# Two of eight batches get their transposed x from VectorE block turns of a second copy, and the whole order is searched anew

## The chip, the cores and the metric

One NeuronCore of one Trainium2 chip runs the kernel as one launch. The metric is the device time of one execution in microseconds (us). Engines are named as the profile names them: PE (TensorE matmul), PEld (its weight load), DVE (VectorE), ACT (ScalarE), POOL (GpSimd), SP (SyncE, which here only issues DMAs).

## What is computed

```python
# x: (8, 8, 512, 64) f32   state: (8, 8, 32, 64) f32
scores = x @ state^T / 8;   a  = softmax(scores);   xread = a @ state
scores2 = state @ x^T / 8;  a2 = softmax(scores2);  sread = a2 @ x
rows = concat([xread, sread], axis=2)          # per batch 544 rows of 8 * 64 = 512
# mixture of depths, per batch:
s = rows @ w_gate                              # 544 scores
top = the 128 rows with the largest s
out[top] = rows[top] + sigmoid(s[top]) * (relu(rows[top] @ w1) @ w2)   # w1: 512x1024, w2: 1024x512
out[others] = rows[others]
```

Both scores of a batch come from one product, x times state transposed; its two softmaxes run along its two axes.

## The kernel before

All work is recorded as 769 pieces by `add(engine, length, fn, after=..., takes=..., uses=...)`. A piece is a few instructions on one engine, with the pieces it needs and the buffers it takes or uses. `carry_out()` then issues the pieces in the order of the table `PLAN`: an entry `122:0:2` is piece 122, its first choice of engine, and buffer number 2 for what it takes. An entry `w:9:7` issues nine "identity turns": transposes of the identity matrix into PSUM bank 7 whose result nobody reads. Each engine runs its own instructions strictly in that order, and waits where an input is not ready. The lengths given to `add` are not used at run time.

Per batch, `attention(b)` does this:

- `load_x` brings x of the batch into one of the `xf` buffers (two DMAs of 512 KB on SP). x is needed in two forms: as it lies (in `state_read`, line 681), and turned, so that the head dimension lies on the partitions (in `scores`, line 516).
- `turn` (line 492) turns x on PE, four 128x128 transposes for each of the four pairs of heads, into a PSUM bank, and `keep` copies the bank into an `xT` buffer, on ACT (line 499) or DVE (line 497).
- `scores` (line 516) makes the scores in two PSUM banks. DVE takes the maximum along one axis (`s_max`, line 546), turns the scores in blocks of 32x32 into `e` (`turn_in`, line 531), takes the other maximum (`x_max`, 534), subtracts (`x_sub`, 537), and after ACT's exponential turns back into `eT` (`turn_out`, 543).
- `read` (line 620, twice per batch) makes xread; `keep` scales it into `xs`, per half a DVE piece of one instruction (line 631) or an ACT piece of eight (line 636); SP stores it (line 645). `turn_a`, `keep_a` and `state_read` (lines 662, 668, 681) make sread; SP stores it (line 691).

`choice(b)` then ranks the 544 scores (`row_x` 738, `win` 754, `wins_over` 779, `one_hot` 788, `pick` 806), fetches the 128 chosen rows by an indirect DMA on POOL (`fetch`, 816) and makes the sigmoid. `layers` runs the two layers for batches 0 and 7 alone (lines 905, 925), and `layers_of_two` for the pairs (1,2), (3,4), (5,6) with seven products of half matrices in place of eight (lines 992, 1099), for which POOL forms sums of the weights (line 415). `put` adds the results to the rows in `out` by an indirect DMA on POOL (line 868).

`ON_DVE` names batches whose x is to be turned by DVE, and is empty before. For such a batch `load_x2` brings a second copy of x by four SP DMAs, each into 32 partitions, in runs of 32 elements (128 bytes) so that 32x32 block turns (`turn_blocks`, four per batch, 512 columns each) give `xT` directly; `turn` and its `keep` fall away.

The state of all batches lies in one buffer, `stb`. Before, it holds one of the five `xf` buffers until the last reader of it is done.

Of the kernel before, what the change touches and what calls it, by code (L numbers as in the profile page):

```python
# [8 lines left out]
F32 = mybir.dt.float32  # L9
# [10 lines left out]
0:0:0 16:0:0 1:0:1 4:0: 3:0: 5:0: 2:0: 11:0: 7:0:2 6:0: 8:0: 20:0: 9:0:3 w:10:7 42:0:0 44:0:1 10:0: 43:0: 17:0: 14:0:  # L20
45:1:0 50:0:2 12:0:4 51:0:1 48:0:0 13:0: 49:1:2 46:0:1 18:0: 47:0:3 w:4:7 52:0:0 21:0: 57:0: 19:0: w:6:7 122:0:2 22:0:
53:0:0 182:0:3 24:0: 123:0:0 25:0: 124:0:4 54:0: 58:0:0 w:2:7 126:0:2 59:0: 55:0: 125:0:1 w:5:7 76:0:0 74:0:1 30:0:
56:0: 26:0: 128:0:4 61:0: 183:0: 60:0:0 129:0:2 77:0:0 27:0: w:9:7 68:0:4 31:0: 127:0:3 28:0: 75:0:1 184:0:0 69:0:
130:0:2 70:0: 185:0:4 71:1:0 78:0:0 135:0: 72:0: 190:0:1 372:0:1 131:0:0 35:0: 191:0:0 w:2:7 62:0:4 73:0: 79:0: 132:0:
136:0:0 188:0:1 80:0: 186:0:0 81:0: 189:0:1 63:0: 36:0: 64:0: 187:0:2 65:1:1 137:0: w:7:3 192:0:0 133:0: 66:0: 370:0:2
34:0: 82:0:3 139:0: 83:0: 193:0:1 152:0:3 134:0: 310:0:4 67:0: 373:0: 84:0:6 197:0: 85:0: 153:0:0 23:0: 154:0:5 91:0:
374:0:3 86:0:0 155:0:1 371:0: 314:0:5 87:0: 156:0:2 315:0:0 88:0: 198:0:0 89:0: 556:0:2 90:0: 138:0:0 199:0: w:2:7
92:0:5 15:0: 312:0:6 375:0:1 214:0:7 93:0: 94:0:0 215:0:0 194:0: w:3:7 95:0:5 157:0: 308:0:7 313:0:2 158:0: 146:0:0
97:0: 309:0:3 195:0: 98:0:0 96:0: 378:0:6 311:0:4 216:0:7 147:0: 99:0: 316:0:4 217:0:1 149:1:0 196:0: 148:0: 376:0:7
150:1: 379:0:0 321:0: w:2:6 140:0:0 377:0:2 558:0:6 141:0: 322:0:0 218:0:7 143:1:1 559:0:3 40:0: 142:0: 679:0:3 323:0:  # L30
# [13 lines left out]
401:1:0 570:0: w:4:3 326:0:0 402:1: 403:0: 283:0:4 327:0: 328:0: 284:0: 574:0:0 412:0:5 348:0:6 289:0:0 413:0: 278:0:2  # L44
# [28 lines left out]
def kernel(  # L73
# [37 lines left out]
    ON_DVE = ()  # L111
# [51 lines left out]
    def add(engine, length, fn, after=(), takes=(), uses=(), key=(), lands=0.0, moves=0.0):  # L163
        options = [(engine, length)] if isinstance(engine, str) else list(zip(engine, length))
        go = (lambda e: fn()) if isinstance(engine, str) else fn
        pieces.append(Piece(options, go, after, takes, uses, key, lands, moves))
        return pieces[-1]
# [38 lines left out]
    R_X = Ring("xf", [128, H, NC, D], F32, 5)  # L206
# [108 lines left out]
    def load_x(b, pieces=2):  # L315
        buf = xf[b] = Buf(R_X)
        n = H // pieces
        p_x[b] = []
        for h in range(0, H, n):

            on = "ACT" if b == 0 and h + n == H else "SP"

            def go(h=h, on=on):
                queue = nc.scalar if on == "ACT" else nc.sync
                queue.dma_start(out=buf.ap[:, h:h + n], in_=x[b, h:h + n].rearrange("h (p c) d -> p h c d", c=NC))

            p_x[b].append(add(on, 0.6, go, takes=[] if h else [buf], uses=[buf] if h else [], key=(b, "load_x"),
                              lands=2.0, moves=3.3 / pieces))
# [138 lines left out]
    def attention(b):  # L467

        def key(n):
            return (b, n)  # L470
# [121 lines left out]
        else:  # L592
            p = add("DVE", 1.25, turn_in, after=[p_s], takes=[e], uses=[s], key=key("in"))
            p = add("DVE", 1.2, x_max, after=[p] + four_ago, uses=[e], key=key("max"))
            p = add("DVE", 1.22, x_sub, after=[p], uses=[e], key=key("sub"))
# [114 lines left out]
    def choice(b, p_sc, p_xt, p_st):  # L710

        def key(n):
            return (b, n)
# [83 lines left out]
        for k, (lo, hi) in enumerate(slot_tiles):  # L797
# [55 lines left out]
            u["got"] = add("POOL", 1.25, fetch, after=[p] + all_stores, takes=[u["xr"]], key=key("fetch"), lands=3.0, moves=0.9)  # L853
# [351 lines left out]
```

## Time and profile before

| | |
|---|---|
| runs shown | 212.14, 215.03, 216.16 us; median 215.03 |
| profiled execution | 213.38 us, of which the span from the first to the last instruction is 211.6 us |
| mean granted PE clock | 0.990 |
| busy in the span | PE 196.9, PEld 169.4, DVE 143.3, ACT 95.4, POOL 81.6 us |

Busy time of PE is modelled from the starts of pipelined matmuls, so stretches are compared by when PE moves on, and by what its idle time waited for.

### The profile page before, as it was taken

The page shows a single profiled execution, that of the slowest core. Times are in us where ns is not written, and L with a number is a line of the kernel's source. Part 1 is how long each engine was busy: PE and PEld are TensorE (multiplying, and loading weights), DVE is VectorE, ACT ScalarE, POOL GpSimd, SP SyncE. Part 2 cuts the span into 40 slices and gives each one's busy share as a digit, 9 for nine tenths or more (in the row PEclk, how much of TensorE's full clock was granted, in tenths as well). Part 3 has the DMA queues.
Part 4 walks back from the last instruction along what each step waited for, and adds up shares of the span by engine and source line. Part 5 has one row for each costly group of instructions (what it writes and reads, how often), then busy time and mean ns, then how long its engine had stood idle before and what let it go on. Part 6 is the DMA issues. An engine that isn't in the chain of part 4 may idle for free.

```text
span 211.6 us, 6083 instructions
## 1 busy us (share of the span) xinstructions
PE 196.9 (93%) x2472; PEld 169.4 (80%) x2472; DVE 143.3 (68%) x378; ACT 95.4 (45%) x266; POOL 81.6 (39%) x174
## 2 busy tenths in 40 slices
PE   5988889887999999999999999999999999999990
PEld 4976657776987587998887889998888898989980
DVE  0389999879979978778977896798778342621000
ACT  2347876776276656213626776474133222130200
POOL 8220970507704839910521530500325327015404
PEclk9999999999699999999999999999999999999999
DMA  6999745969843301322231440431334303494501
GB/s 192 297 370 383 262 126 166 288 213 292 290 133 113 135 12 41 50 103 102 104 112 53 149 65 15 112 84 61 136 127 149 50 5 58 62 304 100 74 0 50
DMA packets 20324, 28.77 MB, mean 136 GB/s; under 512 B 5384, under 2 KB 14856, under 8 KB 20296
## 3 DMA queue, kind: packets, MB, share of 16 engines
q1 hardware_dynamic: 17344, 23.73, 33.5%
q0 software_dynamic: 1888, 4.20, 10.7%
q10 hardware_dynamic: 1064, 0.46, 0.8%
q8 instruction: 19, 0.31, 0.6%
q14 instruction: 9, 0.07, 0.1%
HBM read 17.37 MB, written 11.01 MB: 134 GB/s over the span
## 4 chain that ended last, share of the span: by engine, by line
PE 75%; DVE 8%; issue 7%; ACT 4%; DMA 2%; POOL 2%; POOLq 1%; ACTq 0%; DVEq 0%
PE ps L992 19%; PE ps L1099 18%; PE ps L620 7%; PE ps L492 6%; PE ps L905 5%; PE ps L925 3%; PE ps L516 3%; PE ps L681 2%; PE ps L662 2%; DMA xf_s<-in_state_dram 2%; PE ps L738 2%; PE ps L879 2%; PE ps L779 2%; PE ps L177 2%; DVE state_g_s L368 1%
## 5 line engine op out<-in xcount | busy, mean ns | idle before, releaser
L636 ACT ACTIVATE xs_s<-ps,numbers 128x64 f32<-128x64 f32 x104 | 22.6, 344 | 12.0 <-DVE xs_s L631 6.2
L868 POOL DMA_INDIRECT out_dram<-ot_s,indices x10 | 15.1, 1508 | 22.9 <-ACT ot_s L1125 10.0
L816 POOL DMA_INDIRECT xr_s<-out_dram,indices x8 | 9.5, 1190 | 36.6 <-DVE indices L810 26.7
L499 ACT COPY xT_s<-ps 128x512 f32<-128x512 f32 x29 | 16.5, 589 | 13.8 <-PE ps L492 12.2
L492 PE MATMUL ps<-ident,xf_s 128*128 128x128 f32 x128 | 20.4, 297 | 0.3 <-ACT aT_s L668 0.3
L620 PE MATMUL ps<-st_v,eT_s 32*128 32x66 f32 x512 | 17.9, 276 | 2.3 <-DVE eT_s L543 1.0
L620 PEld LDWEIGHTS ps<-st_v,eT_s 32*128 32x128 f32 x512 | 15.8, 186 | 4.8 <-issue 2.4
L754 DVE SCALAR_TENSOR_TENSOR win_s<-ps,sc,after 128x544 bf16<-128x544 f32 (+4 forms) x40 | 18.1, 508 | 0.7 <-PE ps L741 0.7
L492 PEld LDWEIGHTS ps<-ident,xf_s 128*128 128x128 f32 x128 | 15.7, 152 | 2.2 <-ACT aT_s L668 0.9
L905 PE MATMUL ps<-xg_s,w 128*128 128x128 f32 x128 | 17.1, 296 | 0.0
L905 PEld LDWEIGHTS ps<-xg_s,w 128*128 128x128 f32 x128 | 16.4, 209 | 0.6 <-ACT hT_s L909 0.4
L925 PE MATMUL ps<-w,hT_s 128*128 128x256 f32 (+1 forms) x48 | 14.7, 457 | 0.0
L177 PE MATMUL ps<-ident 128*128 128x128 f32 x56 | 9.6, 308 | 4.4 <-ACT a_s L550 1.5
L764 POOL CAST aux<-sc 128x5 bf16<-128x5 f32 x8 | 2.0, 253 | 29.6 <-DVE sc L727 20.5
L668 ACT COPY aT_s<-ps 128x512 f32<-128x512 f32 x16 | 9.5, 592 | 8.4 <-PE ps L662 7.1
L631 DVE TENSOR_TENSOR xs_s<-ps,numbers 128x512 f32<-128x512 f32 x19 | 12.8, 683 | 0.3
L992 PE MATMUL ps<-xg_s,w1s 128*128 128x128 f32 x96 | 12.5, 280 | 0.2 <-ACT xg_s L886 0.2
L1099 PE MATMUL ps<-w,hT_s 128*128 128x256 f32 x48 | 12.1, 389 | 0.0
L992 PE MATMUL ps<-xc_s,w 128*128 128x128 f32 x96 | 12.1, 279 | 0.0
L1099 PE MATMUL ps<-w,hs_s 128*128 128x256 f32 x48 | 12.1, 388 | 0.0
L177 PEld LDWEIGHTS ps<-ident 128*128 128x128 f32 x56 | 7.3, 159 | 5.8 <-ACT a_s L550 1.7
L992 PEld LDWEIGHTS ps<-xg_s,w1s 128*128 128x128 f32 x96 | 11.3, 191 | 0.6 <-ACT xg_s L886 0.5
(126 smaller groups left out, 445.5 us busy)
## 6 DMA issues: line engine op xcount, KB each, us to landing
out_dram<-xs_s SPq DMA_DIRECT2D x16, 512.0 KB
xf_s<-in_x_dram SPq DMA_DIRECT2D x14, 512.0 KB
w<-in_moe_w_dram SPq DMA_DIRECT2D x2, 2048.0 KB
w<-in_moe_w_dram SPq DMA_DIRECT2D x4, 512.0 KB
xf_s<-in_x_dram SPq DMA_DIRECT2D x3, 256.0 KB
out_dram<-xt SPq DMA_DIRECT2D x16, 32.0 KB
xf_s<-in_state_dram SPq DMA_DIRECT2D x1, 384.0 KB
xf_s<-in_x_dram ACTq DMA_DIRECT2D x1, 256.0 KB
```

The source lines that it names most:

```text
L177: nc.tensor.transpose(P.give(int(places), 1)[:, 0:128], ident, ident)
L492: nc.tensor.transpose(v[:, k, r], xf[b].ap[:, 2 * pair + k, 2 * r:2 * r + 2].rearrange("p w d -> p (w d)"), ident)
L499: nc.scalar.copy(out=t.ap, in_=v)
L620: nc.tensor.matmul(view(o)[:, q, c - c0, g], eT.ap[r, c % 2, g, c // 2], st_v[r, b, g], start=True, stop=True)
L631: nc.vector.tensor_tensor(out=to, in0=of.rearrange("p q g m -> p g q m"), in1=sums[:, c0 + c].unsqueeze(3).to_broadcast([128, 2, 4, D]), o ...
L636: nc.scalar.activation(out=to[:, g, q], in_=of[:, q, g], func=AF.Copy, scale=sums[:, c0 + c, g, q:q + 1])
L754: nc.vector.scalar_tensor_tensor(win_of(c, n), srow.ap[0:n, f:SP], sc[0:n, b, c:c + 1], after[0:n, 0:SP - f], op0=ALU.is_gt, op1=ALU.mult, ...
L868: touches(b, nc.gpsimd.indirect_dma_start(out=flat_out.rearrange("r (n m) -> (r n) m", n=n), out_offset=bass.IndirectOffsetOnAxis(ap=ix[0: ...
L905: nc.tensor.matmul(ph.ap.rearrange("p (f s) -> p f s", f=4)[:, f, 0:m], w1[:, j, 128 * (f0 + f):128 * (f0 + f + 1)], xg.ap[:, j, 0:m], sta ...
L925: nc.tensor.matmul(py.ap[0:m, part], hT[f // 4].ap[:, f % 4, 0:m], w2[:, f, part], start=(f == 0), stop=(f == NF - 1))
L992: nc.tensor.matmul(v[:, f, 0:m], weights[:, j, 128 * f:128 * (f + 1)], moving()[:, j], start=fresh and f == 0 and j == 0, stop=j == 1, ski ...
L1099: nc.tensor.matmul(bank.ap[0:m, 0:256], turned.ap[:, f, 0:m], weights[:, f], start=fresh and f == 0, stop=f == 3, skip_group_check=True)
```

## The change

- `ON_DVE` becomes batches 6 and 7. Their 8 `turn` pieces on PE (32 transposes) and the 8 copies to `xT` go; 8 `load_x2` DMAs on SP and 8 `turn_blocks` pieces on DVE come.
- The second copies need a buffer of their own (`R_X2`, as large as one `xf` buffer). The ring of `xf` shrinks from five to four buffers, and the state lies at first in the `R_X2` buffer. So the first `load_x2` of batch 6 waits for the last reader of the state, and those of batch 7 for the block turns of batch 6.
- `PLAN` is replaced. Identity turns: 56 before (10 of them at the very start), 69 now (14 at the start), the other 55 in short groups before the first layer of batch 0. Attention now runs through the batches in the order 0 to 7 (5 came after 6 and 7 before). Four of the scaling pieces of xread go from DVE to ACT (13 of 32 there before, 17 now), one copy of the turned rows goes from ACT to DVE, `w2` is loaded ahead of `w1`, and ACT's small `first_exp` goes from the start to a late place.

```diff
 PLAN = """
-0:0:0 16:0:0 1:0:1 4:0: 3:0: 5:0: 2:0: 11:0: 7:0:2 6:0: 8:0: 20:0: 9:0:3 w:10:7 42:0:0 44:0:1 ...
+16:0:0 0:0:0 1:0:0 4:0: 2:0: 6:0: 3:0: 7:0:1 20:0: 8:0: w:14:7 44:0:0 17:0: 42:0:1 ...
...
-    ON_DVE = ()
+    ON_DVE = (6,7)
...
-    R_X = Ring("xf", [128, H, NC, D], F32, 5)
+    R_X = Ring("xf", [128, H, NC, D], F32, 4)
     R_X2 = Ring("x2", [128, 2, H, 4, 32], F32, 1) if ON_DVE else R_X
...
-            p_x[b].append(add(on, 0.6, go, ...
+            p_x[b].append(add(on, 0.5 if b != 1 else 1.9 if h == 0 else 2.3, go, ...
...
-            p = add("DVE", 1.22, x_sub, after=[p], uses=[e], key=key("sub"))
+            p = add("DVE", 1.4 if b < 4 else 1.25, x_sub, after=[p], uses=[e], key=key("sub"))
...
-            u["got"] = add("POOL", 1.25, fetch, ..., lands=3.0, moves=0.9)
+            u["got"] = add("POOL", 1.25, fetch, ..., lands=1.8, moves=0.9)
```

The functions that become live:

```python
    def load_x2(b):
        buf = x2[b] = Buf(R_X2)
        ...
                def go(w=w, e=e):
                    src = x[b].rearrange("h (s t r w) (e d) -> w e t r h s d", s=4, t=32, r=2, e=2)[w, e]
                    o = 32 * (2 * w + e)
                    nc.sync.dma_start(out=buf.ap[o:o + 32], in_=src)
...
                def turn_blocks(pair=pair, t=t):
                    nc.vector.transpose(out=t.ap.rearrange("p k r t -> p r k t"),
                                        in_=x2[b].ap[:, :, 2 * pair:2 * pair + 2].rearrange("p r k s d -> p r k (s d)"))
```

In the kernel after, lines behind the table stand one number higher (the first layer of batch 0 is line 905 before and 906 after).

First place: PE ahead of the first layer of batch 0 (`ps<-xg_s_88,w_108`). Before, these rows end in a `read` of batch 2 (`ps<-st_v,eT_s_77`), for which PE waits:

```order
L724 MATMUL ps<-numbers,same_n 32x1
L879 MATMUL ps<-ident,xr_s_85 128x128 x4
L681 MATMUL ps<-xf_s_68,aT_s_79 32x64 x16
L681 MATMUL ps<-xf_s_68,aT_s_80 32x64 x16
L741 MATMUL ps<-ident,sc 128x32
L620 MATMUL ps<-st_v,eT_s_77 128x66 x16
L905 MATMUL ps<-xg_s_88,w_108 128x128 x12
```

After, PE has by then also turned x of batch 5 (`xf_s_65`), and the last thing ahead of the layer is the row of scores of batch 1 (lines 739 and 742):

```order
L493 MATMUL ps<-ident,xf_s_65 128x128 x4
L178 MATMUL ps<-ident 128x128 x2
L621 MATMUL ps<-st_v,eT_s_78 128x66 x16
L663 MATMUL ps<-ident,a_s_76 128x128 x4
L880 MATMUL ps<-ident,xr_s_85 128x128 x4
L178 MATMUL ps<-ident 128x128 x2
L739 MATMUL ps<-ident,sc 128x128 x4
L742 MATMUL ps<-ident,sc 128x32
L906 MATMUL ps<-xg_s_88,w_108 128x128 x16
```

The first `read` of batch 2 has moved behind the first half of the layer, and the scores of batch 4 and the turns of batch 5 have moved ahead of it.

Second place: SP's queue. After, the loads of the second copies (`x_s_68<-in_x_dram`, of batch 6 first, and from the fifth row on of batch 7) stand between stores (`out_dram<-xs_s` for xread, `out_dram<-xt` for sread):

```order
L646 DMA out_dram<-xs_s_82 128x1024
L692 DMA out_dram<-xt 4x32x64 x2
L339 DMA x_s_68<-in_x_dram 32x64x32 x2
L646 DMA out_dram<-xs_s_81 128x1024
L339 DMA x_s_68<-in_x_dram 32x64x32
L646 DMA out_dram<-xs_s_82 128x1024
L339 DMA x_s_68<-in_x_dram 32x64x32 x2
L692 DMA out_dram<-xt 4x32x64 x2
```

The third and fourth load of batch 6 stand right behind the store of sread of batch 4; the first load of batch 7 waits for the fourth block turn of batch 6 and holds up the store behind it meanwhile. Before, this stretch holds stores and plain x loads only.

Third place: DVE where x of batch 6 is turned in blocks (line 481), after. `xd_s` and `xc_s` are operands of the layers of batches 1 and 2:

```order
L970 TENSOR_TENSOR xd_s_92<-ps,xg_s_88 128x256
L538 TENSOR_TENSOR e_s_74<-e_s_74,numbers 128x1024
L641 TENSOR_TENSOR numbers<-ps,numbers 128x16
L643 TENSOR_REDUCE sc<-numbers 128x2
L632 TENSOR_TENSOR xs_s_81<-ps,numbers 128x512
L481 STREAM_TRANSPOSE xT_s_69<-x_s_68 128x2x2x128
L728 COPY sc<-ps 32x1
L481 STREAM_TRANSPOSE xT_s_70<-x_s_68 128x2x2x128
L626 TENSOR_SCALAR numbers<-ps 128x16
```

The four block turns stand among pieces of batches 1 to 5; before, DVE held three copies of turned x in the whole program (line 497) and no block turn of x.

More of the change, by code (lines that the diff above doesn't have):

```diff
@@ L19 @@
 PLAN = """
[L20 to L29, printed above, removed]
@@ L30 @@
-150:1: 379:0:0 321:0: w:2:6 140:0:0 377:0:2 558:0:6 141:0: 322:0:0 218:0:7 143:1:1 559:0:3 40:0: 142:0: 679:0:3 323:0:
[13 rows of a table removed]
-401:1:0 570:0: w:4:3 326:0:0 402:1: 403:0: 283:0:4 327:0: 328:0: 284:0: 574:0:0 412:0:5 348:0:6 289:0:0 413:0: 278:0:2
[24 rows of a table removed]
+16:0:0 0:0:0 1:0:0 4:0: 2:0: 6:0: 3:0: 7:0:1 20:0: 8:0: w:14:7 44:0:0 17:0: 42:0:1 45:1:0 50:0:2 43:0: 51:1:1 w:1:7
+46:0:0 11:0: 22:0: 9:0:2 47:1:2 10:0: w:4:7 48:0:1 18:0: 12:0:3 26:0: 49:0:3 27:0: 13:0: w:6:7 52:0:0 15:0: 122:0:2
+53:0:0 124:0:3 123:0:0 128:0:4 125:0:1 126:0:5 57:0: 129:0:2 54:0: 58:0:0 21:0: 127:0:3 19:0: 55:0: 59:0: w:12:7
@@ new lines @@
+130:0:2 24:0: 61:0: 182:0:0 56:0: 29:0: 184:0:1 131:0:1 74:0:4 183:0: 186:0:5 75:0:0 135:0: 76:0:0 187:0:0 310:0:4
+185:0:1 190:0:5 132:0: 188:0:6 77:0:1 311:0:2 w:1:4 78:0:7 133:0: 189:0:3 191:0:4 372:0:0 31:0: 373:0: 136:0:0 w:5:6
+192:0:0 60:0:0 79:0: 137:0: 197:0: 80:0: w:2:7 62:0:4 134:0: 154:0:2 139:0: 193:0:0 14:0: 152:0:3 155:0:0 38:0:
+153:0:1 w:3:3 368:0:2 63:0: 198:0:0 156:0:3 65:1:0 81:0: 199:0: 194:0: 494:0:1 37:0: 157:0: w:5:3 216:0:0 64:0: 369:0:
+82:0:1 308:0:3 138:0:1 66:0: 214:0:2 83:0: 195:0: w:3:7 312:0:1 25:0: 23:0: 215:0:0 w:1:7 68:0:4 67:0: 309:0:0 30:0:
@@ new lines @@
+32:0: 314:0:2 217:0:1 159:0: 69:0: 370:0:3 313:0:1 70:0: 371:0: 71:1:1 w:2:3 84:0:0 91:0: 315:0:3 85:0: 72:1: 378:0:3
+34:0: 86:0:0 w:1:7 316:0:4 73:0: 379:0:4 495:0: 196:0: 87:0: 158:0: 160:0:2 380:0:3 161:0: 374:0:6 88:0: 218:0:2 89:0:
+375:0:0 90:0: 381:0:1 201:0: 376:0:6 321:0: 92:0:7 377:0:2 w:1:6 382:0:0 93:0: 322:0:0 94:0:0 498:0:3 323:0: 387:0:
+496:0:6 95:0:7 219:0: 317:0:1 499:0:0 w:2:5 340:0:2 96:0: 338:0:3 497:0:1 97:0: 325:0: 339:0:0 98:0:0 w:1:7 140:0:4
+200:0:0 341:0:1 388:0:0 342:0:2 40:0: 141:0: 142:0: 500:0:3 143:1:0 343:0: 389:0: w:1:2 502:0:2 344:0: 144:1: 99:0:
@@ L69 @@
+28:0: w:2:7 146:0:4 501:0:2 383:0:0 503:0:3 145:0: 404:0:3 556:0:2 147:0: 35:0: 104:0:2 405:0:0 148:0: 318:0: 105:0:0
+w:2:3 162:0:0 163:0: 149:0:1 106:0:2 391:0: 33:0: 169:0: 107:0: 164:0:0 558:0:0 150:0: 108:0: 165:0: 220:0: 36:0:
[35 rows of a table added]
 """
@@ L325, in go @@
                 queue.dma_start(out=buf.ap[:, h:h + n], in_=x[b, h:h + n].rearrange("h (p c) d -> p h c d", c=NC))
-            p_x[b].append(add(on, 0.6, go, takes=[] if h else [buf], uses=[buf] if h else [], key=(b, "load_x"),
+            p_x[b].append(add(on, 0.5 if b != 1 else 1.9 if h == 0 else 2.3, go, takes=[] if h else [buf], uses=[buf] if h else [], key=(b, "load_x"),
                               lands=2.0, moves=3.3 / pieces))
@@ L852, in choice @@
             all_stores.extend(p_st if (lo, hi) == slot_tiles[0] else [])
-            u["got"] = add("POOL", 1.25, fetch, after=[p] + all_stores, takes=[u["xr"]], key=key("fetch"), lands=3.0, moves=0.9)
+            u["got"] = add("POOL", 1.25, fetch, after=[p] + all_stores, takes=[u["xr"]], key=key("fetch"), lands=1.8, moves=0.9)
             q = add("POOL", 1.62, below, after=[q], key=key("below"))
```

72 rows, old and new, of the table PLAN are left out of this document.

## The prediction

> **What bounds the kernel now.** I read the page first: the busy times, then the row of PE over the span's 40 slices and the row of its granted clock.
>
> ```profile
> PE 196.9 (93%) x2472; PEld 169.4 (80%) x2472; DVE 143.3 (68%) x378; ACT 95.4 (45%) x266; POOL 81.6 (39%) x174
> PE   5988889887999999999999999999999999999990
> PEclk9999999999699999999999999999999999999999
> ```
>
> PE is nearly the whole span; its gaps all lie in the first ten slices (53 us), and the clock falls once, at the end of them. The PE timeline shows where this first stage ends and where the program ends:
>
> ```profile
> 1.34 2.40 PE L177 MATMUL ps<-ident 128*128 128x128 f32 x10 [1.34 <-POOL ident masks.py:199]
> 4.78 1.12 PE L385 MATMUL ps<-ident,xf_s 128*128 128x128 f32 x4 [1.04 <-DVE xf_s L280]
> 52.27 1.12 PE L620 MATMUL ps<-st_v,eT_s 32*128 32x66 f32 x32 [1.00 <-DVE eT_s L543]
> 53.32 4.57 PE L905 MATMUL ps<-xg_s,w 128*128 128x128 f32 x24
> 199.32 7.17 PE L925 MATMUL ps<-w,hT_s 128*128 128x256 f32 x32
> ```
>
> At 53.3 us PE starts the first layer of batch 0 (L905), and its last product ends at 199.32 + 7.17 = 206.5. So I cut the span at these two points and asked for the busy time of each stretch (columns: length, then busy PE, PEld, DVE, ACT, POOL):
>
> ```profile
> 0.00:53.30 53.30, 44.13 (x766) 36.50 (x766) 40.41 (x98) 32.91 (x77) 23.65 (x48) 1.00 0.81 259
> 53.30:206.50 153.20, 152.76 (x1710) 132.90 (x1706) 102.40 (x280) 62.49 (x189) 55.98 (x124) 0.99 0.35 96
> 10.00:53.30 43.30, 36.51 (x732) 29.58 (x730) 38.35 (x92) 29.66 (x72) 18.59 (x31) 1.00 0.79 263
> ```
>
> The program has **two stages**. In the second PE waits 0.4 us in 153.2: only less PE work shortens it. In the first PE idles 9.2 us, and from 10 us on DVE is the fullest engine, 38.35 of 43.3 us; the read at 52.27, the last wait ahead of the layers, waited for DVE. So 211.6 = 53.3 + 153.2 + a tail of 5.1 (the last add and two scatters), and the execution was 1.8 us longer than its span (213.38). The runs' median, 215.03, is 0.8% above this execution; I sum against the execution.
>
> **The change, part by part.** First the PE work behind the first stage's end. Prices from the chain that ended last:
>
> ```profile
> 73.64 0.87 PE ps L492 x8
> 136.05 1.05 PE ps L620 x32
> 121.00 1.02 PE ps L516 x32
> 127.42 0.44 PE ps L662 x4
> 79.74 1.72 PE ps L925 x4
> 81.45 1.78 PE ps L992 x16
> ```
>
> Before, 11 `turn` pieces of four transposes stand behind the first layer's start (four each of batches 5 and 7, three of 6). After, none: those of 6 and 7 are gone, those of 5 stand ahead. That is 11 × 0.435 = 4.8 us less. One read more stands behind (+1.05), one scores product (−1.02) and one turn of a (−0.44) less. Stage two loses **5.2 us** and would be 148.0.
>
> Second, the clock. Four rows of 2 us each, the granted clock third from the end, and one early stretch with the same idleness:
>
> ```profile
> 26.00:28.00 2.00, 0.74 (x7) 0.75 (x7) 1.93 (x5) 1.98 (x8) 2.00 (x2) 1.00 0.28 72
> 28.00:30.00 2.00, 2.00 (x41) 1.04 (x39) 1.58 (x3) 1.85 (x6) 1.39 (x3) 1.00 0.08 31
> 50.00:52.00 2.00, 0.78 (x41) 0.51 (x29) 1.93 (x8) 1.43 (x3) 0.95 (x5) 1.00 0.88 260
> 52.00:54.00 2.00, 1.73 (x36) 1.69 (x37) 2.00 (x2) 0.00 (x0) 2.00 (x2) 0.91 0.87 237
> 54.00:56.00 2.00, 2.00 (x12) 2.00 (x10) 1.97 (x7) 0.61 (x3) 0.99 (x3) 0.50 0.94 328
> 56.00:58.00 2.00, 2.00 (x15) 2.00 (x15) 1.90 (x12) 0.59 (x3) 1.92 (x1) 0.74 0.73 250
> ```
>
> After PE idled for 1.2 of 2 us the clock fell to half, and 2 × (0.09 + 0.50 + 0.26) = 1.7 us of stage two were lost. The same idleness at 26 to 28 us cost nothing, so the fall is not sure to come with a pause. The 13 further identity turns fill pauses; whether they spare the fall I can't read from one execution. Bounds 0 and 1.7; with no row nearer to either I take half, 0.85. Stage two: **147.1** (146.3 to 148.0).
>
> [...]
>
> Third, the end of the first stage. What DVE must have done by then, from the DVE orders: before all up to `turn_out` of batch 2, after all up to the second gate of batch 1 (for which the row of scores ahead of the layer waits). After, this holds one `s_max`, one `turn_in` and one copy of turned x more, and one scaling piece less. By the groups, with shapes kept apart:
>
> ```profile
> L546 DVE TENSOR_REDUCE numbers<-ps 128x2 f32<-128x1024 f32 x8 | 9.7, 1212 | 2.9 <-PE ps L516 2.9
> L531 DVE STREAM_TRANSPOSE e_s<-ps 128x1024 f32<-128x1024 f32 x8 | 9.9, 1236 | 0.0
> L497 DVE COPY xT_s<-ps 128x512 f32<-128x512 f32 x3 | 2.1, 689 | 3.2 <-PE ps L492 3.2
> L631 DVE TENSOR_TENSOR xs_s<-ps,numbers 128x512 f32<-128x512 f32 x19 | 12.8, 683 | 0.3
> ```
>
> 1.21 + 1.24 + 0.69 − 0.68 = 2.5 us more; some pieces of under 0.7 us each stay in the range. If DVE idles as before, the layer starts at 53.3 + 2.5 = 55.8. If DVE idled nowhere after 10 us, at 10 + 38.35 + 2.5 = 50.8. Neither extreme is likely. The new order puts all of batch 1's DVE chain ahead of batch 0's `turn_out`, which gives DVE work where it waited, but part of its busy time is itself waiting on POOL, and the same six weight sums stay in this stage:
>
> ```profile
> 52.02 2.35 POOL L415 TENSOR_TENSOR w2s<-w 128x1024 f32<-128x1024 f32 x1
> 52.06 2.32 DVE L554 TENSOR_SCALAR numbers<-numbers 128x2 f32<-128x2 f32 x1
> ```
>
> A DVE instruction on two columns lasted as long as POOL's sum beside it. I take **55.0**, near the end that resembles the row before. The four more identity turns at the start cost nothing: 14 × 0.24 from 1.34 end at 4.7, when PE waited for the state (4.78). The early loads move no less data, so this head stays.
>
> Fourth, what the DVE turns cost. A block turn of 512 columns is not in the trace; L531 takes 1236 ns for twice the columns, so 0.62 us. Bounds: 0.62, and 1.24 if the strided pattern halves the rate; I take 0.62, the nearest form. Eight are 4.9 us, the copy moved from ACT 0.7, and four scaling pieces of 0.68 leave: DVE gains 2.9 us, in stage two, where it has 153.2 − 102.4 = 50.8 us free. That covers it, unless a block turn stands ahead of something PE waits for: then up to 2.9 us (6 with the slow turn). ACT:
>
> ```profile
> L499 ACT COPY xT_s<-ps 128x512 f32<-128x512 f32 x29 | 16.5, 589 | 13.8 <-PE ps L492 12.2
> 27.23 1.75 ACT L636 ACTIVATE xs_s<-ps,numbers 128x64 f32<-128x64 f32 x8
> ```
>
> Nine copies of 0.59 go, four scaling pieces of 1.75 come: +1.7 us on an engine that has 90 us free in stage two. Each keeps its PSUM banks 1.1 us longer than DVE would; nothing is charged.
>
> Fifth, the second copies: eight loads of 2048 packets of 128 bytes. No such packet is in the trace. The nearest rows are the queues', with packets, bytes and time:
>
> ```profile
> q1 hardware_dynamic: 17344, 23.73, 33.5%
> q10 hardware_dynamic: 1064, 0.46, 0.8%
> ```
>
> ACT's queue (q10), half of whose packets are 256-byte pieces of the state: 0.008 × 16 × 211.6 us / 1064 = 25 ns per packet of 432 bytes on average. SP's queue: 0.335 × 16 × 211.6 / 17344 = 65 ns for 1368 bytes on average. A 128-byte packet should lie at or below the first, which I take: 2048 × 25 / 16 engines = 3.2 us per load, 26 us for all eight, in a stretch where the DMA engines are 0.35 busy. The tight pair is the third and fourth load of batch 6, issued behind the store of sread of batch 4. From that product to the scores of batch 6, PE's order holds about 17 us (six first-layer pieces of 1.78/2, three second-layer pieces of 1.72, two reads of 1.05, and some 4 us of smaller ones); the four block turns and what stands among them take about 4 of these, so the loads have some 12 us. Two need 6.4 and the latency of landing. **Nothing** is charged. SP's extra issues fall into its idle time.
>
> [...]
>
> **Sum:** 55.0 + 147.1 + 5.1 = 207.2 us of span, + 1.8 = **209.0 us**, 2.1% under the profiled 213.38 and 2.8% under the median.
>
> **The rivals.** *The work only moves* (chance 0.33): DVE idles as before (55.8), the clock falls again (148.0), and the 2.9 us on DVE show as waits on PE: 55.8 + 148.0 + 2.9 + 5.1 + 1.8 = 213.6, no change. For it: DVE is 89% busy from 10 us to the first layer, and the block turns stand between operands (xd, xc) of the pair layers. Against it: the 3.5 us of the 32 removed turns (32 × 0.109) are PE work in the stage where PE never waits.
>
> *The loads of small runs come late* (chance 0.13): at the 65 ns of SP's mean, a load takes 8.3 us. The pair of batch 6 needs 16.6 against 12 (4.6 late), and batch 7's four, issued only after batch 6's block turns, 33 us against about 25 to their own block turns (8 late). DVE waits at the block turn in its order; behind it stand the operands of the pair layers, so PE waits too: 209.0 + 12.6 = 221.6, slower than before. It decides from 12 × 16 / 4096 = 47 ns per packet on, less what landing takes. For it: the four loads of batch 7 can't start early, as the buffer is shared, and a store stands behind the waiting load. Against it: the 25 ns row.
>
> That the identity turns *don't do what they say*, because they stand ahead of ready work instead of in pauses, is a case of the first rival: it would push the layer's start back by up to 55 × 0.11 = 6 us if none of them met a pause, and gives 215 at the worst.
>
> **How the numbers follow.** Forecast 0.54, no change 0.33, late loads 0.13. The forecast's own range is 50.8 + 146.3 + 6.9 = 204.0 to 55.8 + 148.0 + 6.9 = 210.7. The range that should hold 8 in 10 reaches from 204 over the first rival to 216.5. A measurement of this kernel tells about 2% from no change: under 210.7 is faster, over 219.3 slower, against 215.03. Faster 0.54, within 2% 0.32, slower 0.14.
>
> **What would show it.** L905's successor starts at about 55 us; PE is busy from there to the end, 147 us later; no clock row under 1.0 behind 50 us; block turns of about 0.62 us that wait for no DMA; POOL sums that stretch DVE's small instructions as before. A wait of DVE for the second copies, or PE gaps behind the first layer, make it wrong upward; a start of the layer near 51 us, downward.

## The result, and the profile after

The kernel after takes **204.45 us** (median of 4 runs, 204.04 to 204.76), the kernel before 214.52 us beside it (median of 4 runs). The ratio is 0.9565, 95% interval 0.9481 to 0.9649: faster by 4.3%. On a second chip it was 205.71 against 214.35 us, 0.9582 (0.9545 to 0.9619). The forecast was 209.0 us, the range 204.0 to 216.5; the time lies 0.45 us above its lower end.

From the page of after, the busy times, PE's row and its granted clock:

```profile
PE 191.5 (94%) x2453; PEld 165.1 (81%) x2453; DVE 142.5 (70%) x383; ACT 96.6 (48%) x289; POOL 83.2 (41%) x174
PE   7999988979999999999999999999999999999990
PEclk9999999999999999999999999999999999999998
```

The gaps still lie in the first ten slices, and the clock no longer falls. The PE timeline gives the cut between the two stages:

```profile
53.02 3.84 PE L906 MATMUL ps<-xg_s,w 128*128 128x128 f32 x32
```

The same two stretches as in the prediction (length, then busy PE, PEld, DVE, ACT, POOL):

```profile
0.00:53.00 53.00, 47.12 (x799) 38.90 (x799) 40.90 (x107) 33.68 (x80) 23.90 (x48) 1.00 0.78 254
53.00:197.40 144.40, 144.35 (x1655) 126.18 (x1654) 101.16 (x278) 62.94 (x211) 58.20 (x125) 1.00 0.47 119
```

The span is 53.0 + 144.4 + 5.3 = 202.7 us. So the first stage is as long as before (53.3), and nearly the whole gain, 8.8 us, lies in stage two, where PE waits for 0.05 us. Against the forecast (55.0, 147.1, 5.1) both stages came out shorter, by 2.0 and 2.7 us. The clock stays up across pauses nearly as deep as the one ahead of its fall before: in the rows below PE idles 0.85 and 0.49 us, before it was 1.22 and 0.27 us in 50 to 54 us (granted clock third from the end):

```profile
42.00:44.00 2.00, 1.15 (x13) 1.03 (x13) 1.95 (x2) 1.52 (x5) 0.00 (x0) 1.00 0.00 0
44.00:46.00 2.00, 1.51 (x16) 1.35 (x19) 1.85 (x5) 0.17 (x1) 1.22 (x1) 1.00 0.00 0
```

DVE's groups of after (mean ns behind the comma, then the idle time before them):

```profile
L481 DVE STREAM_TRANSPOSE xT_s<-x_s 128x512 f32<-128x512 f32 x8 | 5.4, 690 | 0.0
L719 DVE SCALAR_TENSOR_TENSOR state_g_s<-xt,wg_s 128x128 f32<-128x128 f32 x8 | 3.1, 392 | 0.1
```

A block turn takes 0.69 us and never waits for its load. The other is one of the small instructions that stood beside GpSimd's sums before, a piece of the gate's scores. Before, its row read:

```profile
L718 DVE SCALAR_TENSOR_TENSOR state_g_s<-xt,wg_s 128x128 f32<-128x128 f32 x8 | 4.5, 557 | 0.6 <-ACT xt L686 0.5
```

From the page, SP's queue (packets, MB, share of the time of 16 DMA engines):

```profile
q1 hardware_dynamic: 33856, 25.82, 41.4%
```

### The profile page after: what moved, and what is told of

It reads as the page before. It is cut to its first block, busy times and chain, and to the rows that moved or that the text cites. A ratio compares the mean times of both kernels' runs of the same rounds, so it can differ in the third digit from the quotient of the medians.

```text
span 202.7 us, 6083 instructions
## 1 busy us (share of the span) xinstructions
PE 191.5 (94%) x2453; PEld 165.1 (81%) x2453; DVE 142.5 (70%) x383; ACT 96.6 (48%) x289; POOL 83.2 (41%) x174
## 4 chain that ended last, share of the span: by engine, by line
PE 85%; DVE 4%; DMA 3%; ACT 3%; ACTq 1%; issue 1%; POOLq 1%; POOL 0%; DVEq 0%
PE ps L993 20%; PE ps L1100 19%; PE ps L621 8%; PE ps L906 7%; PE ps L926 7%; PE ps L682 4%; DMA wg_s<-in_moe_w_gate_dram 3%; PE ps L663 3%; PE ps L517 3%; PE ps L493 3%; PE ps L178 3%; PE ps L780 2%; PE ps L739 2%; PE ps L880 2%; DVE e_s L532 1%; DVE numbers L547 1%
## 5 line engine op out<-in xcount | busy, mean ns | idle before, releaser
L637 ACT ACTIVATE xs_s<-ps,numbers 128x64 f32<-128x64 f32 x136 | 29.5, 347 | 13.7 <-DVE offs L785 3.9
L178 PE MATMUL ps<-ident 128*128 128x128 f32 x69 | 13.0, 312 | 5.3 <-POOL ident masks.py:199 1.3
L906 PE MATMUL ps<-xg_s,w 128*128 128x128 f32 x128 | 15.2, 277 | 0.0
L493 PE MATMUL ps<-ident,xf_s 128*128 128x128 f32 x96 | 14.6, 290 | 0.4 <-ACT xT_s L500 0.4
L500 ACT COPY xT_s<-ps 128x512 f32<-128x512 f32 x21 | 11.8, 593 | 6.5 <-PE ps L493 5.7
L493 PEld LDWEIGHTS ps<-ident,xf_s 128*128 128x128 f32 x96 | 11.2, 148 | 1.9 <-issue 0.8
L993 PE MATMUL ps<-xc_s,w 128*128 128x128 f32 x96 | 12.6, 277 | 0.0
L1100 PE MATMUL ps<-w2s,hT_s 128*128 128x256 f32 x48 | 12.1, 388 | 0.0
L551 ACT ACTIVATE a_s<-ps,numbers 128x512 f32<-128x512 f32 x16 | 11.0, 693 | 2.1 <-DVE numbers L547 2.1
L993 PEld LDWEIGHTS ps<-xc_s,w 128*128 128x128 f32 x96 | 11.7, 192 | 0.2
L416 POOL TENSOR_TENSOR w<-w 128x1024 f32<-128x1024 f32 x4 | 10.9, 2891 | 2.2 <-PE ps L906 2.2
```

The lines of the kernel that those rows point to most:

```text
L178: nc.tensor.transpose(P.give(int(places), 1)[:, 0:128], ident, ident)
L493: nc.tensor.transpose(v[:, k, r], xf[b].ap[:, 2 * pair + k, 2 * r:2 * r + 2].rearrange("p w d -> p (w d)"), ident)
L500: nc.scalar.copy(out=t.ap, in_=v)
L551: nc.scalar.activation(out=a.ap[:, g], in_=view_s()[:, :, g], func=AF.Exp, bias=nm[:, g:g + 1], accum_out=ss[:, g:g + 1])
L637: nc.scalar.activation(out=to[:, g, q], in_=of[:, q, g], func=AF.Copy, scale=sums[:, c0 + c, g, q:q + 1])
L906: nc.tensor.matmul(ph.ap.rearrange("p (f s) -> p f s", f=4)[:, f, 0:m], w1[:, j, 128 * (f0 + f):128 * (f0 + f + 1)], xg.ap[:, j, 0:m], sta ...
```

## The experiments

All ratios are to the kernel before, run beside on the same chip; after's is 0.9565 and 0.9582. The chips differ by up to 2 us (before took 212.56 to 214.54), so ratios are compared, not times.

### x of batches 6 and 7 turned on PE again, in the new order

`turns_back` keeps the order and its identity turns, and `turns_back_2` does the same with the turns better placed. In both, `ON_DVE` is empty, and the block turns give way to `turn` (PE) and its copy:

```diff
-    ON_DVE = (6,7)
+    ON_DVE = ()
 # PLAN of turns_back_2
+558:0:0 559:1:3 ... 562:0:3 563:1:0 560:0:3 561:1:1 564:0:3 565:1:2 ... 685:0:3 686:1:0 687:0:2 688:1:2 ... 681:0:3 682:0:1 ... 683:0:2 684:0:3
 # turns_back_2 alone: five x buffers, as before
-    R_X = Ring("xf", [128, H, NC, D], F32, 4)
+    R_X = Ring("xf", [128, H, NC, D], F32, 5)
```

> The order of after and its identity turns, but x of batches 6 and 7 is turned on PE again: 8 turn pieces and 8 copies (on DVE, in place of the block turns) come back, the second copies are not loaded, the state keeps its own buffer. My theory: PE never waits behind 53 us, so each piece costs its PE time, 0.435 to 0.60 us; with the two batches 3.5 to 4.8 us more than after: 208 to 209.3 us. Rival (the new order and the clock made the whole gain, the block turns only moved work from PE to where it was hidden): within 1 us of after, 204 to 205.5.

It took 212.01 us, 0.9965 (0.9943 to 0.9988): by the ratios (0.9965 - 0.9582) × 212.56 = 8.1 us over after, outside both theories. PE's waits from the first layer on, where after has none:

```profile
PE ps L493 <- ACT xs_s L637: 1.3, 2, 0.8
PE ps L993 <- ACT xs_s L637: 1.1, 1, 1.1
PE ps L880 <- DVE xT_s L498: 0.8, 1, 0.8
```

3.2 us are waits for a PSUM bank that ACT's scaling pieces or the copy still held, so this run mixes the price of the turns with that of their banks. PE's busy time in stage two tells them apart in part: it is 148.56 us against 144.35 of after, 4.2 us more.

> The order of after with x of 6 and 7 turned on PE again, placed better than in the first turned-back kernel: five x buffers as in before, so that x of batch 7 is there early, and each turn into a PSUM bank that has been free for some time. In the first one 3.2 us of its 7.5 us over after were waits of PE for banks around 114 to 124 us. My theory: those go, what stays is the PE time of 32 transposes, 3.5 to 4.8 us over after (0.975 to 0.982 of before). Rival 1 (the new order has no room for the turns, wherever they stand): still 6 us or more over after, 0.985 to 1.0 of before. Rival 2 (order alone is the gain): within 1 us of after, 0.96 of before.

It took 210.37 us, 0.9805 (0.9758 to 0.9852). The waits for banks are gone but for 0.3 us. Its stage two, and the group of the turns in it:

```profile
54.40:204.40 150.00, 149.09 (x1687) 129.38 (x1686) 100.37 (x275) 64.21 (x213) 57.82 (x125) 1.00 0.37 101
```

```profile
L493 PE MATMUL ps<-ident,xf_s 128*128 128x128 f32 x32 | 5.1, 281 | 0.3 <-DVE q_s L1013 0.3
```

Against after, (0.9805 - 0.9582) × 214.4 = **4.8 us** (3.5 to 6.1 with both intervals), as my theory had it. The second rival (within 1 us) falls; the first (6 us or more) lies at the very end of the interval. In the profiled execution, the slowest of the six, stage two is 4.7 to 5.6 us longer than in the two of after (145.3 and 144.4), and 5.1 us is the busy time of the turns. So in the new order the 32 transposes cost about their PE time, 0.13 (by `turns_back`) to 0.17 us each. In this execution the first stage is longer too, 54.4 us instead of 53.0: at 19 us a turn of x waits 1.3 us for a bank where after waits 0.4. The other half of the gain, 1 - 0.9805 or 4.2 us (3.2 to 5.2), belongs to the order and all else that changed, without any block turn.

### The turns left out of the old order

`before_unturned`:

```diff
             def turn(pair=pair, ps=ps):
+                if b in (6, 7):
+                    return
...
             def keep(e, ps=ps, t=t):
+                if b in (6, 7):
+                    return
```

> Before with the 8 turn pieces of batches 6 and 7 and their copies left out and nothing in their place: the scores of these two batches are made from what the buffers held before, so the output of these two batches is not the reference's. It prices the turns alone in the old order. My theory: 8 x 0.435 to 0.60 = 3.5 to 4.8 us less than before. Rival 1 (their copies and banks held PE up too, as in the turned-back kernel, which lost 7.5 us against after): 6 to 8 us less. Rival 2 (hidden): under 1 us.

It took 213.46 us, 0.9944 (0.9908 to 0.998): only 1.2 us less (0.4 to 2.0), near rival 2. Its stage two from the first layer to the end of the last product, and the largest wait in it:

```profile
52.77:204.34 151.57, 148.71 (x1682) 128.43 (x1678) 100.60 (x275) 58.42 (x180) 56.40 (x124) 1.00 0.35 98
```

```profile
PE ps L728 <- DVE state_g_s L722: 0.9, 1, 0.9
```

PE's idle time rose from 153.20 - 152.76 = 0.4 us to 151.57 - 148.71 = 2.9 us. With the turns gone, PE reaches products whose operands DVE and ACT have not finished. This execution is the fastest of the ten (211.2 us, the median is 213.46) and its clock never falls; before's lost 1.7 us of its 153.2 to the fall. At full clock that is 151.5 against 151.57: between these two executions the turns were worth nothing. So leaving the 32 transposes out was worth about 1.2 us in the old order, and they cost about 4.8 in the new one. The parts don't add up: the order without block turns brings 4.2 us, the turns alone 1.2, both together (1 - 0.9582) × 214.4 = 9.0. No run has the block turns themselves in the old order.

### Fewer identity turns

`no_early` keeps the first 14 only, `none` has none, `after_few` has these groups:

```diff
-w:14:7 w:1:7 w:4:7 w:6:7 w:12:7 w:1:4 w:5:6 w:2:7 ... (69 in all)
+w:14:7 w:6:7 w:6:7 w:3:1 w:6:7
```

> After with the 14 identity turns at the start alone; the 55 in short groups of the first stage are left out. Theory 1 (they keep the granted clock up): the clock falls to about half somewhere before or just behind the first layer, stage two or the end of stage one loses 1.7 us or more: 206.2 us or more. Theory 2 (the order itself has no pause that matters): clock stays at 1.00, within 0.5 us of 204.5. Theory 3 (they stand ahead of ready work): 55 x 0.11 = 6 us of PE work leave a stage where PE is 90% busy, the first layer starts 1 to 3 us earlier, 201.5 to 203.5.

It took 202.41 us, 0.9488 (0.9434 to 0.9541): faster than after, so the 55 stand in the way (theory 3), and the first layer starts earlier than at 53.02:

```profile
51.93 3.84 PE L904 MATMUL ps<-xg_s,w 128*128 128x128 f32 x32
```

The PE timeline shows how, first after, with the wait ahead of two identity turns in brackets, then the same place in `no_early`:

```profile
42.80 0.35 PE L807 MATMUL ps<-aux,oh_s 128*128 128x5 bf16 x5
44.49 0.44 PE L178 MATMUL ps<-ident 128*128 128x128 f32 x2 [1.33 <-DVE indices L811]
44.76 1.04 PE L663 MATMUL ps<-ident,a_s 128*128 128x128 f32 x8
```

```profile
43.46 0.35 PE L805 MATMUL ps<-aux,oh_s 128*128 128x5 bf16 x5
43.74 1.09 PE L661 MATMUL ps<-ident,a_s 128*128 128x128 f32 x8
```

These two turns were given bank 5, which held scores of batch 3 until DVE had turned them:

```profile
43.19 1.24 DVE L532 STREAM_TRANSPOSE e_s<-ps 128x1024 f32<-128x1024 f32 x1
```

The turn of a behind them was ready: without them it starts at once. A piece of work that nobody reads waited 1.33 us for its bank here, and held up all of PE's queue. Theory 1 is not wrong either. The profiled execution of `no_early`, 203.44 us, has a fall of the clock:

```profile
26.00:28.00 2.00, 1.19 (x10) 0.94 (x10) 2.00 (x3) 1.08 (x5) 2.00 (x2) 1.00 1.04 395
28.00:30.00 2.00, 0.72 (x7) 0.48 (x5) 1.97 (x6) 1.28 (x7) 2.00 (x4) 1.00 1.04 418
30.00:32.00 2.00, 1.93 (x28) 1.69 (x32) 1.93 (x8) 2.00 (x7) 1.46 (x3) 0.63 1.02 385
32.00:34.00 2.00, 2.00 (x23) 1.88 (x20) 1.60 (x11) 0.41 (x1) 0.20 (x1) 0.50 0.90 332
```

Its six runs lie at 203.3 to 203.4 us with a mean granted clock of 0.981 to 0.982, and at 200.5 to 201.6 with 0.992 to 0.994: the fall costs about 2 us and does not come in each execution.

> After without any identity turn, the 14 at the start left out too. If the start turns cost nothing and only warm the clock: the first x turns run at a lower clock, the first scores come later by at most the difference, 0 to 1 us more than no_early. If they stand in the way, the first x turn (4.38 us in after) starts earlier and the time falls under no_early by up to 0.5 us.

It took 201.43 us, 0.9456 (0.942 to 0.9492), which can't be told from `no_early`: six of its eight runs lie at 200.9 to 201.6 us, two at 203.88 and 205.71. The 14 turns at the start neither cost nor bring anything that these runs can tell: without them the clock of the profiled execution reads 1.00 in each row of 2 us up to 24 us all the same.

> After with 21 identity turns behind the 14 at the start in place of 55: 6 ahead of the scores of batch 1, 6 ahead of a turn that waits for x, 3 and 6 ahead of two rows that wait for DVE, each into a bank whose last reader is long done. Theory 1 (an early identity turn costs time where its bank is still held by an earlier reader, 3.9 us of such waits in after; in a true pause with a free bank it costs nothing and keeps the clock): first layer at 51 us or earlier, clock above 0.99, 200.5 to 201.5 in every run. Theory 2 (every identity turn costs its PE time): about 1 us more than the kernel without the early ones, 202 to 203.5. Theory 3 (the falls of the clock have nothing to do with these pauses): runs still spread from 200.5 to 203.5.

It took 202.19 us beside after's 205.71 on the same chip, 0.9412 (0.9375 to 0.9448), all six runs within 201.8 and 202.84 with clocks of 0.993 to 0.999. That is above the 200.5 to 201.5 that I had written for another chip; on the chip of `no_early`, where before took 212.56, the ratio gives 200.1 us. Theory 1 fits best: beside `no_early`'s 0.9488 the 21 turns cost nothing that shows (theory 2 asked for about 1 us), the first layer starts before 51 us, and the runs spread over 1.0 us in place of 2.9 (on another chip, though). It has **the lowest ratio of all versions**, 1.8% under after's on the same chip (0.9412 / 0.9582); the intervals of `no_early` and `none` touch its own. The PE timeline and stage two:

```profile
50.34 3.84 PE L905 MATMUL ps<-xg_s,w 128*128 128x128 f32 x32
```

```profile
50.30:195.70 145.40, 144.88 (x1655) 126.38 (x1654) 101.39 (x279) 63.66 (x213) 59.64 (x129) 1.00 0.48 119
```

The first stage is 2.7 us shorter than after's; stage two is as long as that of after on this chip (145.3). One of the four groups was placed badly all the same: PE waited 1.8 us ahead of the last six turns, for a bank that ACT's scaling piece still read, and the turn of x behind them starts at 31.39 us, where in `no_early` it starts at 30.07.

### The clock in the old order

`before_warm` puts 13 identity turns, into a free bank, into the two pauses ahead of the old first layer; `before_none` takes all 56 out of the old order.

```diff
 # before_warm
+w:4:4
 163:0: ...
+w:9:4
 202:0:0
```

> Before, with 13 more identity turns in the two pauses ahead of the first layer (4 ahead of the row of scores at 51.0 us, 9 ahead of the read at 52.3 us). If the clock fell because PE paused there: rows behind 52 us keep 1.00, the time falls by 1.7 us to about 212.8 against 214.5. If the fall has another cause: the clock still falls to about 0.50 in 54 to 56 us, change within 0.5 us.

It took 213.32 us, 1.0025 (0.9995 to 1.0055). The clock row that had read 0.50, and the PE timeline:

```profile
54.00:56.00 2.00, 2.00 (x40) 1.93 (x35) 1.80 (x11) 0.32 (x2) 2.00 (x3) 1.00 1.03 324
```

```profile
52.46 1.20 PE L177 MATMUL ps<-ident 128*128 128x128 f32 x9
53.59 1.12 PE L620 MATMUL ps<-st_v,eT_s 32*128 32x66 f32 x32
54.64 1.60 PE L905 MATMUL ps<-xg_s,w 128*128 128x128 f32 x12
```

The clock was kept, but the first layer starts at 54.64 instead of 53.32: in this execution what was saved in clock was given back in PE's queue. The nine turns outlast their pause, and the read behind them starts at 53.59 instead of 52.27.

> Before without any identity turn (56 go). If identity turns stand in the way in that order as they do in after: 1 to 3 us faster than before. If the granted clock needs them there: slower, by 1 to 4 us. If neither: within 1 us.

It took 213.96 us, 0.9972 (0.9947 to 0.9996): the third case. The first layer starts earlier, but the clock falls twice, for 10.2 us from about 25 us on, and again in stage two, where PE stands after the first products (this execution is 1.7 us over the median; the mean clock of all 14 runs is 0.963 to 0.990):

```profile
52.61 2.94 PE L905 MATMUL ps<-xg_s,w 128*128 128x128 f32 x24
```

```profile
56.00:58.00 2.00, 0.51 (x14) 0.38 (x11) 2.00 (x1) 0.96 (x5) 1.98 (x1) 1.00 0.96 338
58.00:60.00 2.00, 1.81 (x18) 1.57 (x26) 1.31 (x7) 0.09 (x1) 0.00 (x0) 0.74 0.91 283
60.00:62.00 2.00, 2.00 (x33) 0.78 (x23) 0.10 (x1) 0.65 (x2) 0.00 (x0) 0.50 0.24 84
```

So all identity turns together cost the new order (0.9582 - 0.9456) × 214.4 = 2.7 us and the old one 0.6 (0.1 to 1.1): what the old order gains without them at the first layer's start it loses again in this pause and in the clock. With the turns placed anew (`after_few`) the new order gains 3.6.

### GpSimd's sums of the weights cut short

`nosums_before` and `nosums_after`. Both also clear the buffers of the sums once, which gives VectorE 2.6 us of work at the very start:

```diff
+                cut = (lambda ap: ap[:, :, 0:8]) if name in ("w1s", "w2s") and op == ALU.add else (lambda ap: ap)
-                (nc.vector if e == "DVE" else nc.gpsimd).tensor_tensor(out=to, in0=one, in1=other, op=op)
+                (nc.vector if e == "DVE" else nc.gpsimd).tensor_tensor(out=cut(to), in0=cut(one), in1=cut(other), op=op)
```

> Before with the six sums of weights that GpSimd forms in the first stage cut to 8 columns of their blocks, so the rest of these sums is missing and the layers of the pairs are not the reference's. If GpSimd's sums stretch VectorE's instructions and the first stage ends by VectorE: 14 us of GpSimd work go, VectorE's two-column instructions of up to 2.3 us shrink to 0.15 to 0.17 us, the first layer starts 2 to 4 us earlier than 53.3 us. If VectorE is not what sets the end of the stage: first layer within 0.5 us.

It took 211.0 us, 0.9844 (0.9783 to 0.9905), 3.3 us less. The first layer starts 2.4 us earlier, and no two-column instruction is stretched any more (min, median and max ns):

```profile
50.89 2.94 PE L909 MATMUL ps<-xg_s,w 128*128 128x128 f32 x24
```

```profile
L558 DVE TENSOR_SCALAR numbers<-numbers x8: 147/159/227, 16.3 to 142.1; 128x2 f32<-128x2 f32 x8
```

Before, the maximum of these eight was 2320 ns. But that one, at 52.06 us, stands behind the last `turn_out`, so the layer doesn't wait for it. What lies on the chain to the layer is a piece of the gate's scores (line 718) beside another sum, and behind it that `turn_out` (the first row is from GpSimd's timeline, the others from the chain that ended last):

```profile
47.85 2.37 POOL L415 TENSOR_TENSOR w2s<-w 128x1024 f32<-128x1024 f32 x1 [5.66 <-DMA w<-in_moe_w_dram]
48.39 2.00 DVE state_g_s L718 x2
50.97 1.16 DVE eT_s L543
```

With the sums cut, the eight pieces of that line take 0.28 us on average (0.56 before). That gives 1.8 of the 2.4 us; the rest had been gained by 44 us. The clock of the four runs is 0.994 to 1.000 beside 0.986 to 0.996 in before's, so part of the 3.3 us may be the clock. In both places VectorE's instruction began behind the start of GpSimd's sum and ended within 0.2 us of its end: 2.32 us beside a sum of 2.35, and 2.00 beside 2.37. By what means the sum holds the instruction up, no run here shows.

> After with the same six sums cut to 8 columns, so the layers of the pairs are not the reference's. In after the two-column instructions already last 153 ns on average, since they stand elsewhere beside the sums. If that is why the first stage held its 53 us in spite of 2.5 us more VectorE work: less to gain than in before, first layer 0 to 1.5 us earlier than 53.0 us. If the sums still stretch VectorE as before: 2 to 4 us earlier.

It took 205.69 us, 0.9587 (0.9529 to 0.9645), the same as after. The first layer does not move:

```profile
53.17 3.06 PE L910 MATMUL ps<-xg_s,w 128*128 128x128 f32 x25
```

In the new order the sums still stretch VectorE, but where the layer doesn't wait: one, right behind the layer's start, holds a piece that multiplies the state by the gate for 2.25 us (minimum, median and maximum of 16 in ns):

```profile
53.03 2.38 POOL L416 TENSOR_TENSOR w1s<-w 128x1024 f32<-128x1024 f32 x1
L369 DVE SCALAR_TENSOR_TENSOR state_g_s<-x_s,wg_s x16: 204/224/2253, 8.6 to 53.2; 128x64 f32<-128x64 f32 x16
```

And VectorE no longer ends the stage. Before, the chain to the layer is VectorE's from 44.7 us to the read at 52.27. After, it leaves VectorE at 44.5 us; from there to the layer it is PE's own queue, identity turns among it, with two pieces of ACT:

```profile
43.27 1.16 DVE e_s L532
44.49 0.44 PE ps L178 x2
52.49 0.44 PE ps L739 x4
```

### Smaller runs in the second copies' loads

`loads_cut`:

```diff
-                    nc.sync.dma_start(out=buf.ap[o:o + 32], in_=src)
+                    for f in range(0, 32, 8):
+                        nc.sync.dma_start(out=buf.ap[o:o + 32, :, :, :, f:f + 8], in_=src[:, :, :, :, f:f + 8])
```

> After with each load of the second copies cut into four, in runs of 32 bytes: 65,536 packets in place of 16,384, the same bytes, four times the issues. In after a 128-byte packet cost about 12.6 ns of a DMA engine (queue's share of busy time against before). If a packet costs by its number: about 50 ns per 128 bytes, which is the point (47 ns) from which I expected PE to wait: 0 to 3 us over after, waits of VectorE for the loads at the block turns of batch 7. If a packet costs by its bytes: no change, within 0.5 us. If SP's issues are what limits: stores come late too, 2 to 6 us over after.

It took 226.25 us, 1.0532 (1.0465 to 1.0598): (1.0532 - 0.9582) × 214.4 = 20.4 us over after, far more than any case had. The block turns' group, the issues of the third and fourth load of batch 6 in SP's timeline, and the queue's row on the page:

```profile
L482 DVE STREAM_TRANSPOSE xT_s<-x_s 128x512 f32<-128x512 f32 x8 | 5.3, 690 | 10.3 <-DMA x_s<-in_x_dram 10.3
```

```profile
75.62 12.83 SPq L340 DMA_DIRECT2D x_s<-in_x_dram  x8
```

```profile
q1 hardware_dynamic: 83392, 25.83, 47.8%
```

VectorE waited 10.3 us at batch 6's first block turn: the rival of the late loads, at the first of the two places that the prediction had named. By the queue's share of time against before, a packet of 32 bytes cost about (0.478 × 16 × 225.5 - 0.335 × 16 × 211.6) / 66048 = 8.9 ns, so 36 ns per 128 bytes, under the 47 ns from which I expected it. But eight issues kept SP's queue for 12.83 us, 1.6 us each; after needed 2.40 us for the same two loads. Stores behind the loads came late too, as in the third case: VectorE waited 6.1 us for one to free an `xs` buffer. PE stood behind both waits:

```profile
DVE xs_s L633 <- DMA out_dram<-xs_s: 7.4, 2, 6.1
PE ps L881 <- DVE sc L729: 7.0, 1, 7.0
PE ps L808 <- DVE oh_s L790: 5.5, 1, 5.5
```

In stage two of this execution (53.2 to 220.0 us) PE is busy for 152.55 us and idle for 14.3, where after has 144.35 and 0.05, and the mean clock is 0.94. So of the loss there some 14 us are waits and some 8 a lower clock. Whether the issues were slow by themselves or because the queue was full stays open.

## Why the prediction was right, and where its sum was off

The direction, the place (PE's work in stage two) and the range were right; the sum was 4.5 us too high. That the time lies in the range is in part luck: stage two, 144.4 us (145.3 on the second chip), came out under the lowest that I gave it, 146.3, and the total stays over 204.0 only because the first stage was 2.2 us above its own lower bound, and for another reason than I had given.

- **PE work behind the first layer's start, 5.2 us less: right in kind, too small.** I priced a turn piece at 0.435 us by eight transposes that run on without a break. Turned back, eight pieces cost 4.8 us by the ratios, 0.60 each (0.53 by PE's time in `turns_back`, 0.64 by the turns' busy time in `turns_back_2`). The group of before's turns in stage two already said 6.3 / 44 = 0.143 us a transpose, 0.57 a piece:

```profile
L492 PE MATMUL ps<-ident,xf_s 128*128 128x128 f32 x44 | 6.3, 279 | 0.0
```

  With 0.60, 11 pieces are 6.6 us instead of 4.8: 1.8 of the 2.7 us by which stage two came out shorter (1.8 on the second chip).
- **The clock, half of 1.7 us: it was all of it.** No profiled execution of after shows the fall, which gives another 0.85 us. Together that is 2.65 of 2.7 us; that it closes so well is partly chance, since between 0.53 and 0.64 a piece the 11 pieces differ by 1.2 us. The clock doesn't need 55 further identity turns: 21 keep it too (0.993 to 0.999 in the six runs of `after_few`).
- **The first stage, 55.0 us: measured 53.0, and near it by chance.** The step that failed is that DVE's queue ends this stage: after, the chain to the layer leaves DVE at 44.5 us, and PE's queue ends it. DVE's busy time ahead of the layer grew by 0.5 us and not by 2.5 (40.41 to 40.90), as the sums stretch less of it there (of the two-column instructions the longest lasts 0.16 us instead of 2.32), and PE's grew by 3.0 (44.13 to 47.12). "POOL sums that stretch DVE's small instructions as before" came, but off the chain: the sums cost the old first stage 2.4 us and the new one nothing. That the further identity turns fill pauses failed for many of the early ones: with 34 fewer the layer starts 2.7 us earlier. It then starts at 50.34, close to the lower bound, 50.8 with DVE never idle; but DVE still idles 2.7 us there from 10 us on (37.61 busy of 40.30), so that is no proof of the bound.
- **DVE's added work of 2.9 us is hidden: right.** A block turn takes 0.69 us instead of 0.62, none waits for its load, and PE idles for 0.05 us behind the first layer's start (0.5 on the second chip).
- **The loads cost nothing: right, by a smaller price.** (0.414 × 16 × 202.7 - 0.335 × 16 × 211.6) / 16512 = 12.6 ns for a packet of 128 bytes by this estimate, half of the 25 that I took. The point from which the rival decides was wrong: it reckoned packets alone and left out how long SP's queue is held by each issue (1.2 us in after's third and fourth load, 1.6 in those of `loads_cut`).
- **The rivals.** "The work only moves" didn't come, but it describes the old order well: there the turns that were left out turned into 2.5 us of waits. Its case of identity turns ahead of ready work came in part, 2.7 of the 6 us that I gave it at most. What the forecast lacked is that the order and the block turns depend on each other. It gave the order the turns of batch 5 that stand ahead (4 × 0.435 = 1.7 us) and half of the clock's fall, and took 1.7 us for the longer first stage; the order brought 4.2 us without block turns.

## What to carry to other kernels

Work taken off the busiest engine pays only as far as the order behind it has operands ready (the 32 transposes were worth 1.2 us in the old order and 4.8 in the new one): price it in the order that it will run in, and search the order again after taking it out. Fill work for a clock needs a buffer that has long been free (PE waited 1.33 us for one that was not) and must end before the next operand comes (nine turns that did not held the read back by 1.3 us); take it out and time it again whenever the order changes. The engine whose work ended a stage in the old order need not end it in the new one: ask for the chain before you add to its sum. For a price, take the duration that a piece costs where it stands alone between other pieces (here 0.60 us), not its share of a long run (0.435).

## What the runs showed of the hardware

- The granted clock fell in some executions of one program and not in others (`no_early`: three runs of six with a mean of 0.981 to 0.982, three with 0.992 to 0.994), and between `no_early` and `after_few` the depth of a pause didn't decide it. PE idled 0.81 and 1.28 us in two neighbouring rows of 2 us of `no_early` and the clock went to 0.50; it idled 1.13 and 0.68 us in `after_few`, 1.81 us of it in one piece, and the clock stayed:

```profile
28.00:30.00 2.00, 0.87 (x8) 0.63 (x6) 1.97 (x4) 1.13 (x6) 2.00 (x2) 1.00 1.03 416
30.00:32.00 2.00, 1.32 (x14) 1.16 (x14) 1.93 (x8) 2.00 (x7) 1.61 (x4) 1.00 1.02 386
```

- Four falls lasted about 3.4, 3.4, 6.8 and 10.2 us, estimated as time at half clock from the clock in rows of 2 us: (0.09 + 0.50 + 0.26) × 2 / 0.5 = 3.4 us in before, 3.4 in the second fall of `before_none` (0.74, 0.50 and 0.90), 6.8 in `no_early` (0.63, 0.50, 0.50 and 0.66) and 10.2 in the first fall of `before_none` (0.71, four times 0.50, and 0.73). What starts a fall these runs don't show. PE was busy for part of each row ahead of one: 0.78 of 2 us in before, 0.72 in `no_early`, 0.94 and 0.51 in `before_none`.
- Estimated from the queue's share of time, cutting packets from 128 to 32 bytes lowered the price of a packet only from 12.6 to 8.9 ns, so the same bytes cost 2.8 times as much.
